# Head loads from two queues, small loads and constants later, and expert 0's W2 split moved behind attention

## The chip, the cores and the metric

One core of one Trainium2 chip. The time is that of the whole kernel on the device, in microseconds (us); of several runs the median is given, and one further execution is taken with the hardware profiler. Engines are called by their names or as the profile does: PE is TensorE's matmul, PEld its weight load, DVE VectorE, ACT ScalarE, POOL GpSimd, SP SyncE; a q behind the name is the engine's sequencer, which issues DMAs.

## The reference, cut to what matters

A linear attention with decay (state of 48 x 48 per head, 4 sequences of 768 tokens, 8 heads) gives x, and x goes through a mixture of 8 experts, two for each token:

```
for t in range(S):
    cur = einsum('bhd,bhe->bhde', u * k[t], v[t])
    y[t] = einsum('bhd,bhde->bhe', r[t], state + cur)
    state = w * state + einsum('bhd,bhe->bhde', k[t], v[t])
x = y as [3072, 384]
noisy = x @ w_gate + log1p(exp(x @ w_noise)) * noise
top 2 of 8 experts a token, weights by softmax over the two
out[token] += weight * (relu(x @ w1[e]) @ w2[e])     # w1 384 x 1024, w2 1024 x 384
```

All in float32.

## The kernel before, in words

**Attention.** 24 tiles of 128 tokens: step i of the loop `for i in range(NT)` handles chunk i // 4 of sequence i % 4. For a tile r and k are transposed and scaled by powers of w (`trans`; r's result is rT, multiplied on VectorE, k's is kT, copied on ScalarE), multiplied to scores (`scores`, line 415) and masked on VectorE onto a tile that holds the diagonal (`mask`, line 420). The diagonal is the sum of r k u over a head: GpSimd forms the product (`uterm_a`, two operations of 384 columns, lines 376 and 378), VectorE sums it (`uterm_b`, line 386), GpSimd and ScalarE write it into place (`diag`, a select on line 392 and four activations). GpSimd also prepares k for the state update (`prep_k`, two operations of 192 columns, line 370). `kvup` and `zadd` update the state, `inter` and `intra` (lines 464 and 477) multiply scores and state with r and v, `back` and `xout` transpose the result and store x to DRAM. Chunk 5 has no state update. Step i works on tile i and prepares i + 1 and i + 2.

**Order.** The kernel is scheduled by hand: each engine and each DMA queue runs its instructions in the order in which the program writes them. Loads are all issued by SyncE, `load(i + 4)` in step i; the program's first lines load tiles 0 to 2, u, the gate weights (`wg`, four small loads) and the noise (`nz`, four). `consts_a` writes small constants, on GpSimd and VectorE, ahead of the loop.

**Routing.** Every fourth tile's logits are taken (`logits`, line 520). The tokens fall into two groups, of tiles 0 to 12 and 13 to 23. When a group's logits are there, `route(g)` is queued: some hundred short VectorE operations, of which `rstep(us)` issues a measured share at two places in a step; what the first group works on is in PSUM where possible, the second group's operands are in SBUF. `consts_c` checks w (five VectorE operations on one partition) in steps 17 and 19. From the lists that come out GpSimd gathers rows of x by indirect DMA (`xgather`, line 982; `gate0` for the weights, line 1026).

**Experts.** A weight matrix is split into a high part (`w_hi`, ScalarE) and a low part, the matrix less the high part (`w_lo`, VectorE, line 345), and each product is made of three matmuls. Expert 0's seven blocks (three of W1 of 1024 columns, four of W2 of 768) pass through three staging buffers during attention. Block j is loaded in step `W0_AT[j] - 1`, split high in `W0_AT[j] + 2` and low in `W0_AT[j] + 3`:

```
W0_AT = (3, 6, 8, 10, 12, 14, 16)
W_LAG = 2
```

so loads are in steps 2, 5, 7, 9, 11, 13 and 15, high parts in 5 to 18, low parts in 6, 9, 11, 13, 15, 17 and 19. After attention `p1(0, 0)` (line 1080) and `p2(0, 0)` (line 1116) run expert 0 on its first three tiles of tokens, beside the second routing pass; then the other chunks and experts follow.

## Time and profile before

| | us |
|---|---|
| median of three runs | 590.85 (587.71 to 591.36) |
| the profiled execution | 582.96 |
| its span, first to last instruction | 581.2 |

| engine | busy us | share of the span | instructions |
|---|---|---|---|
| PE | 558.4 | 96% | 4460 |
| PEld | 526.7 | 91% | 4461 |
| DVE | 351.3 | 60% | 818 |
| POOL | 268.9 | 46% | 375 |
| ACT | 240.8 | 41% | 559 |

The span falls into the head (to about 28 us), attention (to about 140 us) and the experts. Matmuls are pipelined, so a busy PE need not be at its peak, and the granted clock of a stretch says at which of its speeds TensorE ran, 1.00 being full. The spans on POOL are rough. A share over the whole span is an average over stages with different limits.

### The profile page before, as it was taken

Reading aid. Unit: us, or ns where it says so; the run is one execution under the profiler, and the core shown is the slowest. Engines: PE = TensorE matmul, PEld = TensorE weight load, DVE = VectorE, ACT = ScalarE, POOL = GpSimd, SP = SyncE. Lnnn points to the kernel's source line nnn. Section 1 sums busy time; section 2 is a strip of 40 time slices with the busy share of each in tenths; the row PEclk is TensorE's granted clock in tenths of the full one; section 3 lists DMA queues with packets and bytes.
Section 4 is the critical chain, followed back from the end, with each engine's and each line's share of the span. In section 5 each row is a group of like instructions: output and inputs, shape, how many; then the busy total and the mean of one; then the engine's idle time right before and its main releaser. Section 6 shows DMA issues by size and latency. Waiting matters only on the chain.

```text
span 581.2 us, 12332 instructions
## 1 busy us (share of the span) xinstructions
PE 558.4 (96%) x4460; PEld 526.7 (91%) x4461; DVE 351.3 (60%) x818; ACT 240.8 (41%) x559; POOL 268.9 (46%) x375
## 2 busy tenths in 40 slices
PE   6999998989989999999999999999999999999995
PEld 3788886877979899999999999999999999999994
DVE  7567879968959885636373646455453745455330
ACT  3576767644225251524342444334342533434220
POOL 6789767672036375136322633371445146235102
PEclk9999999979999999999999999999999999999998
DMA  9999998747624266456553835483546448554101
GB/s 126 180 207 220 210 211 178 149 125 213 214 49 129 90 163 161 127 150 171 145 154 110 208 108 165 117 213 103 165 127 186 126 133 212 137 160 119 43 15 40
DMA packets 133816, 85.13 MB, mean 146 GB/s; under 512 B 109522, under 2 KB 123907, under 8 KB 133748
## 3 DMA queue, kind: packets, MB, share of 16 engines
q1 hardware_dynamic: 124196, 56.38, 41.3%
q0 software_dynamic: 9552, 27.89, 16.4%
q8 instruction: 37, 0.61, 0.5%
q14 instruction: 31, 0.25, 0.2%
HBM read 57.89 MB, written 19.37 MB: 133 GB/s over the span
## 4 chain that ended last, share of the span: by engine, by line
PE 83%; DVE 7%; SPq 2%; DMA 2%; issue 2%; POOL 1%; ACT 0%; POOLq 0%; DVEq 0%
PE ph L1080 34%; PE pym L1116 32%; PE pa L415 3%; PE yt L477 3%; PE pt L403 2%; PE yt L464 1%; SPq L135 1%; PE ptb L486 1%; DMA xg<-xd,GR 1%; DVE am L420 1%; PE pym L1107 1%; PE pym L1109 1%; PE pwarm L428 1%; PE pl L520 1%; DMA rd<-in_r_dram 1%
## 5 line engine op out<-in xcount | busy, mean ns | idle before, releaser
L1116 PE MATMUL pym<-w1h,hb 128*128 128x384 f32 x768 | 199.6, 336 | 0.0
L1116 PEld LDWEIGHTS pym<-w1h,hb 128*128 128x128 f32 x768 | 138.9, 188 | 0.1
L1080 PE MATMUL ph<-xh,w0h 128*128 128x384 f32 (+2 forms) x384 | 131.8, 343 | 0.7 <-ACT xh L1055 0.7
L1080 PE MATMUL ph<-xl,w0h 128*128 128x384 f32 (+2 forms) x384 | 131.5, 342 | 0.5 <-DVE xl L1056 0.5
L1080 PE MATMUL ph<-xh,w0l 128*128 128x384 f32 (+2 forms) x384 | 131.3, 342 | 0.0
L1116 PE MATMUL pym<-w1l,hb 128*128 128x384 f32 x384 | 128.9, 336 | 0.0
L1086 DVE SCALAR_TENSOR_TENSOR hb<-ph,hb 128x384 fp32r<-128x384 f32 x128 | 71.0, 555 | 92.2 <-ACT hb L1084 54.9
L1139 POOL DMA_INDIRECT out_dram<-ot,TK x53 | 55.7, 1051 | 138.0 <-DVE ot L1135 122.4
L1084 ACT ACTIVATE hb<-ph 128x384 fp32r<-128x384 f32 x128 | 63.0, 492 | 102.5 <-PE ph L1080 97.8
L1080 PEld LDWEIGHTS ph<-xh,w0h 128*128 128x128 f32 x384 | 72.2, 188 | 1.6 <-ACT xh L1055 0.9
L1080 PEld LDWEIGHTS ph<-xl,w0h 128*128 128x128 f32 x384 | 72.0, 188 | 1.2 <-DVE xl L1056 0.8
L1080 PEld LDWEIGHTS ph<-xh,w0l 128*128 128x128 f32 x384 | 72.1, 188 | 0.6
L1116 PEld LDWEIGHTS pym<-w1l,hb 128*128 128x128 f32 x384 | 72.1, 188 | 0.0
L982 POOL DMA_INDIRECT xgt<-xd,GR x39 | 39.4, 1011 | 68.8 <-DVE ht L1086 36.7
L991 POOL DMA_INDIRECT pv<-out_dram,GA x46 | 51.8, 1126 | 27.5 <-issue 15.4
L1124 ACT ACTIVATE ot<-pym 128x384 f32<-128x384 f32 x39 | 19.2, 492 | 92.6 <-PE pym L1116 80.9
L1056 DVE TENSOR_TENSOR xl<-xq,xh 128x384 fp32r<-128x384 f32 (+2 forms) x39 | 21.0, 539 | 33.9 <-ACT xh L1055 33.9
L420 DVE COPY_PREDICATED am<-mneg,pa 128x512 f32<-128x512 int32 x48 | 32.5, 730 | 13.5 <-PE pa L415 12.2
L1135 DVE SCALAR_TENSOR_TENSOR ot<-ot,GT,pv 128x384 f32<-128x384 f32 (+2 forms) x43 | 25.9, 610 | 16.3 <-ACT ot L1124 16.3
L1055 ACT ACTIVATE xh<-xq 128x384 fp32r<-128x384 f32 (+2 forms) x39 | 19.7, 505 | 32.4 <-DVE xq L1046 27.1
L397 ACT ACTIVATE am<-ident,c 128x128 f32<-128x128 f32 x96 | 30.4, 391 | 1.3 <-DVE c L386 1.3
L345 DVE TENSOR_TENSOR w1l<-stg,w1h 128x768 fp32r<-128x768 f32 x32 | 30.8, 964 | 0.0
(297 smaller groups left out, 766.7 us busy)
## 6 DMA issues: line engine op xcount, KB each, us to landing
stg<-in_moe_w_dram SPq DMA_DIRECT2D x32, 384.0 KB, 4.0
stg<-in_moe_w_dram SPq DMA_DIRECT2D x72, 128.0 KB, 4.1
xq<-xgt SPq DMA_DIRECT2D x176, 36.0 KB, 1.9
rd<-in_r_dram SPq DMA_DIRECT2D x24, 192.0 KB, 4.8
vd<-in_v_dram SPq DMA_DIRECT2D x24, 192.0 KB, 4.6
out_dram<-zrow SPq DMA_DIRECT2D x16, 288.0 KB, 4.6
kt<-in_k_dram SPq DMA_DIRECT2D x23, 192.0 KB, 4.0
stg<-in_moe_w_dram SPq DMA_DIRECT2D x6, 512.0 KB, 5.9
```

Source lines behind the costliest of these rows:

```text
L345: nc.vector.tensor_sub(lo, tv, hi.bitcast(F32))
L397: nc.scalar.activation(AM[i][:, 1, p, :], ident, AF.Copy, scale=C8[i][:, 1, p, :])
L420: nc.vector.copy_predicated(AM[i][:, s], mneg.to_broadcast([128, NP, 128]), PA[i][s])
L982: nc.gpsimd.indirect_dma_start(out=xg[:n], out_offset=None, in_=xd[:GROUPS[GEARLY - 1][1] * 128] if early_ else xd, in_offset=bass.Indirec ...
L991: nc.gpsimd.indirect_dma_start(out=pv[:n], out_offset=None, in_=out, in_offset=bass.IndirectOffsetOnAxis(ap=GA[:n, e * NJ + t:e * NJ + t + ...
L1056: nc.vector.tensor_sub(xl[:, g], v, xh[:, g].bitcast(F32))
L1080: nc.tensor.matmul(ph[:, :w_], a[:, d, fs], x[:, :w_ // 32, d], start=(j == 0), stop=(j == len(q) - 1))
L1084: nc.scalar.activation(h_[:, f, 0, :], ph[:, a:b], AF.Relu)
L1086: nc.vector.scalar_tensor_tensor(h_[:, f, 1, :], ph[:, a:b], 0.0, h_[:, f, 0, :].bitcast(F32), op0=ALU.max, op1=ALU.subtract)
L1116: nc.tensor.matmul(py, hb[:, f, a, hs], x[:, f, :], start=(j == 0), stop=(j == len(q) - 1))
L1135: nc.vector.scalar_tensor_tensor(ot[:n], pt[:n], g, PV[e, t][:n], op0=ALU.mult, op1=ALU.add)
L1139: st = nc.gpsimd.indirect_dma_start(out=out, out_offset=bass.IndirectOffsetOnAxis(ap=TK[:n, q:q + 1], axis=0), in_=ot[:n], in_offset=None, ...
```

## The change

1. Head: the second load of w, that of u and that of tile 0's r are issued by ScalarE, the rest by SyncE. u's broadcast (`pub`, `ub`) comes before the first transposes.
2. The gate weights are loaded in step 1, the noise in steps 8 to 11.
3. GpSimd's order ahead of the loop and in steps 0 to 3: k of tile 1 is prepared before that of tile 0, and in steps up to `HEAD` the product for tile i + 2 comes behind the select of tile i + 1 and the prepared k, not ahead of them. Its sum (`uterm_b`) comes behind the masks.
4. Six VectorE operations of `consts_a` go to the end of step 1 (`consts_b`).
5. The check of w goes from steps 17 and 19 to 8 and 10.
6. Expert 0's blocks have tables of their own: W1's are loaded in steps 4, 7 and 10, W2's in 18, 19, 20 and 22. W2's low parts are made by GpSimd, in steps 22 and 23 and, the last two, after the first step of `p1(0, 0)`, and so is the last high part, on ScalarE.

```
+W0_AT = {4: 0, 7: 1, 10: 2, 18: 3, 19: 4, 20: 5, 22: 6}
+W0_HI = {7: 0, 10: 1, 13: 2, 20: 3, 21: 4, 22: 5}
+W0_LO = {8: 0, 11: 1, 14: 2, 22: 3, 23: 4}
+HEAD = 3
+NZ_AT = 8
-FLAG_AT = 17
+FLAG_AT = 8
...
-        nc.sync.dma_start(wp[two * 64:two * 64 + D, :],
+        (nc.scalar if two else nc.sync).dma_start(wp[two * 64:two * 64 + D, :],
...
-    load(0, (0, 2))
+    load(0, (0, 1))
...
-    nc.sync.dma_start(ur, bass.AP(tensor=u.tensor, offset=u.offset, ap=[[0, 1], [1, H * D]]))
+    nc.scalar.dma_start(ur, bass.AP(tensor=u.tensor, offset=u.offset, ap=[[0, 1], [1, H * D]]))
+    load(0, (1, 2), nc.scalar)
     load(0, (2, 3))
     load(1)
     load(2)
...
-    def w_lo(e, k):
+    def w_lo(e, k, eng=None):
         if e < E:
             tv, hi, lo = w_view(e, k)
-            nc.vector.tensor_sub(lo, tv, hi.bitcast(F32))
+            (eng or nc.vector).tensor_sub(lo, tv, hi.bitcast(F32))
...
+    def consts_b():
+        nc.vector.tensor_scalar(ltri, idif, 0.0, None, op0=ALU.is_gt)
+        nc.vector.tensor_scalar(ier, ie, -1.0, float(E), op0=ALU.mult, op1=ALU.add)
+        nc.vector.tensor_scalar(ie_n[:, 0, :], ie, float(LS), None, op0=ALU.mult)
+        nc.vector.tensor_copy(pid[:, 0, :], ie[:1])
         nc.vector.tensor_copy(imp, im)
         nc.vector.tensor_copy(ijp, ij.rearrange("p e j -> p (e j)")[:, :NJ])
...
     consts_a()
     uterm_a(0)
-    uterm_a(1)
-    prep_k(0)
+    prep_k(1)
     uterm_b(0)
     diag(0, 0)
     diag(0, 1)
-    prep_k(1)
+    uterm_a(1)
+    prep_k(0)
     scores(0)
-    nc.vector.tensor_mul(RKU[1], RKU[1], ub)
     mask(0, 0)
     mask(0, 1)
-    uterm_b(1)
...
             trans(i + 1, 0)
-            if i + 2 < NT:
+            if HEAD < i < NT - 2:
                 uterm_a(i + 2)
+            if i == 0:
+                nc.vector.tensor_mul(RKU[1], RKU[1], ub)
+                uterm_b(1)
+                prep_k(2)
             diag(i + 1, 0)
             trans(i + 1, 1)
-            diag(i + 1, 1)
-        if i - W_LAG - 1 in W0_AT:
-            w_lo(0, W0_AT.index(i - W_LAG - 1))
+            if i:
+                diag(i + 1, 1)
+        if i in W0_LO and i < 20:
+            w_lo(0, W0_LO[i])
         inter(i)
         if i:
             logits(i - 1, wgs)
-        if i + 2 < NT:
+        if 0 < i < NT - 2:
             prep_k(i + 2)
+        if i <= HEAD:
+            uterm_a(i + 2)
         rstep(STEPS_A, False)
...
+        if i in W0_LO and i >= 20:
+            w_lo(0, W0_LO[i], nc.gpsimd)
...
-        kvup(i)
+        if i:
+            kvup(i)
         intra(i)
+        if i == 0:
+            diag(1, 1)
+            kvup(0)
         zadd(i)
-        if i + 2 < NT:
+        if HEAD < i < NT - 2:
             uterm_b(i + 2)
         if nxt:
             scores(i + 1)
             mask(i + 1, 0)
             mask(i + 1, 1)
+        if i <= HEAD:
+            uterm_b(i + 2)
+        if i == 1:
+            consts_b()
...
+        if i == 1:
+            load_wg()
+        if NZ_AT <= i < NZ_AT + B:
+            load_nz(i - NZ_AT)
...
-        if i + 1 in W0_AT:
-            w_load(0, W0_AT.index(i + 1))
+        if i in W0_AT:
+            w_load(0, W0_AT[i])
         back(i)
-        if i - W_LAG in W0_AT:
-            w_hi(0, W0_AT.index(i - W_LAG))
+        if i in W0_HI:
+            w_hi(0, W0_HI[i])
...
     fill(FILL)
+    w_lo(0, 5, nc.gpsimd)
+    w_hi(0, 6)
+    w_lo(0, 6, nc.gpsimd)
```

## Rows read from the trace of the kernel before

**Rows 1.** The chain that ended last, whole kernel: start us, us, what

```profile
15.78 4.76 DMA rd<-in_r_dram
...
29.42 0.89 PE yt L477 x16
...
57.97 0.99 PE yt L464 x16
...
62.90 0.60 PE yt L464 x16
...
119.27 1.98 PE yt L477 x16
...
165.07 4.59 DMA xg<-xd,GR
```

**Rows 2.** Busy us of each engine by stretch, clock, DMA share, GB/s

```profile
core 0: us, PE busy (x) PEld busy (x) DVE busy (x) ACT busy (x) POOL busy (x), PEclk, DMA share, GB/s
28.00:82.00 54.00, 53.95 (x925) 45.92 (x923) 39.30 (x69) 36.65 (x99) 45.94 (x59) 1.00 0.98 213
82.00:128.00 46.00, 40.43 (x643) 34.24 (x645) 41.63 (x102) 28.00 (x81) 31.63 (x45) 0.93 0.67 151
120.00:130.00 10.00, 10.00 (x135) 8.55 (x132) 5.13 (x13) 4.32 (x13) 8.46 (x12) 0.72 0.31 85
```

**Rows 3.** Timeline of the head, SyncE's queue: start us, us, engine, line, operation

```profile
10.38 1.34 SPq L151 DMA_DIRECT2D wg<-in_moe_w_gate_dram  x2
...
12.74 2.22 SPq L155 DMA_DIRECT2D nz<-in_moe_noise_dram  x4
```

**Rows 4.** Timeline of the head, the engines: start us, us, engine, line, operation

```profile
7.49 0.60 ACT L215 ACTIVATE tabk<-ptab 128x512 f32<-128x512 f32 x1 [0.98 <-PE ptab L212]
...
26.44 0.64 POOL L392 TENSOR_SCALAR_AFFINE_SELECT am<-c 128x512 f32<-128x512 f32 x1
26.53 0.55 DVE L386 TENSOR_REDUCE c<-rku 128x8 f32<-128x384 f32 x1 [0.69 <-POOL rku L378]
...
27.05 1.16 POOL L370 TENSOR_TENSOR kd<-kt,tabk 128x192 f32<-128x192 f32 x2
...
28.16 1.00 POOL L376 TENSOR_TENSOR rku<-rd,kt 128x384 f32<-128x384 f32 x1
...
30.19 0.64 POOL L392 TENSOR_SCALAR_AFFINE_SELECT am<-c 128x512 f32<-128x512 f32 x1
...
32.75 0.69 DVE L408 TENSOR_TENSOR rT<-pt,pwr 128x512 f32<-128x512 f32 x1
```

**Rows 5.** Timeline of the routing stage, VectorE, and TensorE behind it

```profile
101.50 1.18 DVE L345 TENSOR_TENSOR w1l<-stg,w1h 128x768 fp32r<-128x768 f32 x1
...
108.80 1.36 DVE L420 COPY_PREDICATED am<-mneg,pa 128x512 f32<-128x512 int32 x2 [0.16 <-PE pa L415]
...
113.28 0.94 DVE L345 TENSOR_TENSOR w1l<-stg,w1h 128x768 fp32r<-128x768 f32 x1
...
116.01 0.34 DVE L289 TENSOR_SCALAR stg<-stg 1x384 f32<-1x384 f32 x1
...
117.71 0.14 DVE L293 CAST tab<-bad 1x1 int32<-1x1 f32 x1
...
119.27 1.98 PE L477 MATMUL yt<-am,vd 128*64 128x128 f32 x16 [2.55 <-DVE am L420]
```

**Rows 6.** Timeline: a VectorE operation beside a GpSimd one, and again alone

```profile
110.51 1.00 POOL L378 TENSOR_TENSOR rku<-rku,ub 128x384 f32<-128x384 f32 x1
...
110.67 0.88 DVE L773 SCALAR_TENSOR_TENSOR r_s<-SLF,r_om 128x13 f32<-128x13 f32 x1
...
158.16 0.18 DVE L773 SCALAR_TENSOR_TENSOR r_s<-SLF,r_om 128x11 f32<-128x11 f32 x1
```

**Rows 7.** Timeline after attention: GpSimd's last gate gather, second routing pass, TensorE

```profile
143.54 0.95 POOL L1026 DMA_INDIRECT GT<-xd,GX  x1 [0.30 <-issue]
...
144.34 0.24 DVE L694 SCALAR_TENSOR_TENSOR r_p<-lg 128x88 f32<-128x88 f32 x1
...
157.25 0.20 PE L758 MATMUL pwarm<-r_om,ltri 128*128 128x88 bf16 x1
```

More of the change, by code (lines that the diff above doesn't have):

```diff
@@ L29 @@
 STEPS_KV = 0.42
-W0_AT = (3, 6, 8, 10, 12, 14, 16)
-W_LAG = 2
+W0_AT = {4: 0, 7: 1, 10: 2, 18: 3, 19: 4, 20: 5, 22: 6}
[3 more added lines that the diff above has]
+NZ_AT = 8
 FILL = 1
 STEPS_END = 0.9
-FLAG_AT = 17
+FLAG_AT = 8
 STEPS_P1 = 0.85
@@ L122, with load @@
     rt, kt, vt = {}, {}, {}
-    def load(i, part=(0, 3)):
+    def load(i, part=(0, 3), eng=None):
         c, b = divmod(i, B)
@@ L134, in load @@
                 t = kd[0][:, :, :D]
-            nc.sync.dma_start(t, src[b, :, c * C:(c + 1) * C, :].rearrange("h t e -> t h e"))
+            (eng or nc.sync).dma_start(t, src[b, :, c * C:(c + 1) * C, :].rearrange("h t e -> t h e"))
             dst[i] = t
-    load(0, (0, 2))
+    load(0, (0, 1))
     ub = const.tile([128, H, D], F32, name="ub")
@@ L148, with load_wg, load_nz @@
     nc.vector.memset(wg, 0.0)
-    for a, src in enumerate((w_gate, w_noise)):
-        for j in range(2):
-            nc.sync.dma_start(wg[j * 64:j * 64 + D, :, a * E:(a + 1) * E],
-                              src.rearrange("(j b d) e -> j d b e", j=2, d=D)[j])
-    nz = const.tile([128, NCH, B, E], F32, name="nz")
-    for b in range(B):
-        nc.sync.dma_start(nz[:, :, b, :], noise[b * S:(b + 1) * S, :].rearrange("(c p) e -> p c e", p=128))
-    nz = nz.rearrange("p c b e -> p (c b) e")
+    def load_wg():
+        for a, src in enumerate((w_gate, w_noise)):
+            for j in range(2):
+                nc.sync.dma_start(wg[j * 64:j * 64 + D, :, a * E:(a + 1) * E],
+                                  src.rearrange("(j b d) e -> j d b e", j=2, d=D)[j])
+    nz4 = const.tile([128, NCH, B, E], F32, name="nz")
+    nz = nz4.rearrange("p c b e -> p (c b) e")
+    def load_nz(b):
+        nc.sync.dma_start(nz4[:, :, b, :], noise[b * S:(b + 1) * S, :].rearrange("(c p) e -> p c e", p=128))
     zrow = const.tile([128, DM], F32, name="zrow")
@@ L197 @@
     nc.scalar.activation(pwr[:, :, 0:64], pwk[:, :, 127:63:-1], AF.Copy)
+    pub = psum.tile([128, H * D], F32, name="pub", tag="py0")
+    nc.tensor.matmul(pub, one_r, ur, start=True, stop=True)
+    nc.scalar.activation(ub.rearrange("p h d -> p (h d)"), pub, AF.Copy)
     kT, rT = {}, {}
@@ L212 @@
         nc.tensor.transpose(ptab[:, p, :], pwk[:, p, :], ident)
-    pub = psum.tile([128, H * D], F32, name="pub", tag="py0")
-    nc.tensor.matmul(pub, one_r, ur, start=True, stop=True)
     nc.scalar.activation(tabk.rearrange("p h d -> p (h d)"), ptab.rearrange("p a b -> p (a b)"), AF.Copy)
-    nc.scalar.activation(ub.rearrange("p h d -> p (h d)"), pub, AF.Copy)
     acc = const.tile([128, E], BF16, name="acc")
@@ L255, in consts_a @@
     def consts_a():
-        nc.vector.tensor_scalar(ltri, idif, 0.0, None, op0=ALU.is_gt)
         nc.gpsimd.memset(ones_b, 1.0)
@@ L263, in consts_a @@
         nc.gpsimd.iota(ie, pattern=[[1, E]], base=0, channel_multiplier=0, allow_small_or_imprecise_dtypes=True)
-        nc.vector.tensor_scalar(ier, ie, -1.0, float(E), op0=ALU.mult, op1=ALU.add)
-        nc.vector.tensor_scalar(ie_n[:, 0, :], ie, float(LS), None, op0=ALU.mult)
         nc.gpsimd.memset(dl, 0.0)
@@ L269, in consts_a @@
         nc.gpsimd.memset(cap[:, E - NS:], float(NM * 128))
-        nc.vector.tensor_copy(pid[:, 0, :], ie[:1])
         nc.gpsimd.iota(im, pattern=[[1, 128]], base=0, channel_multiplier=0)
```

## The prediction

> **What bounds the kernel now.** I read the chain of waits first, as it names the stage in which time can be won, then the busy times by stage, then the timeline of the two stages that the change touches. The chain has four stretches. Up to about 25 us it runs through the load queue: the r tile of step 3 is issued at 15.78 and lands 4.76 us later, and GpSimd stands still for it [rows 1]. From 28 to 82 us the chain is TensorE alone, one tile step in 4.5 us (57.97 to 62.90, less the 0.39 that part 2 explains) [rows 1]. From 82 to 122 us it is VectorE, on which the first routing pass runs beside attention; TensorE is busy 40.43 of 46 us there and its mean clock is 0.93 [rows 2]. After attention it goes to and fro between VectorE's second routing pass, a gather (165.07, 4.59 us) and expert 0's matmuls [rows 1], and from expert 1 on it is matmuls. The change can win only in the first and third stretch, and can lose in the second and fourth.
>
> **1. The head: -0.3 us.** The four small gate loads and the four noise loads hold SyncE's queue from 10.38 to 14.96 [rows 3]. They leave it, and the third tile's loads follow the others directly, so the r that landed at 20.54 should land near 16. The chain of GpSimd then decides, in its new order. The table of powers is ready at 8.09 [rows 4]. Behind it come, in the queue's order, prepared k of tile 1 (1.16), the select of tile 0 (0.64), r times k of tile 1 (1.00), prepared k of tiles 0 and 2 (2.3), the select of tile 1 (0.64); with gaps the product of tile 2 starts at about 14.4. From there every tile up to 5 is one round: in the old order a round, from select to select, takes 3.75 us (26.44 to 30.19), as the sum over the product is taken by VectorE while GpSimd does something else. In the new order the select waits right behind that sum, 0.55 us, and a dispatch, so a round takes 4.4 [rows 4]. Three rounds bring the product of tile 5 to 27.6, its second half and its sum to 30.2, and VectorE's rT of tile 5, which is queued behind that sum, to some 30.8, against 32.75 [rows 4]: a gain of 1.9. Against it stands the block of small constants that moves from before the tiles to step 1. Its four VectorE operations within SBUF come just when GpSimd works without a gap, and such an operation waits until GpSimd's running instruction is over (part 5): four waits of 0.4 to 1.0, about 2 us, of which I take 1.6 as lying on the chain, since rT of tile 3 and the masks are queued behind them. Net -0.3. Bounds: -3.0 (the constants find gaps, the product of tile 2 starts a microsecond earlier) and +2.0 (they find none, and TensorE, idle between the masks, drops to its lower clock for a tile). Issue on ScalarE's queue saves SyncE some 0.6 us an issue [rows 3], which is inside these 1.9; wp, u and r of tile 0 take ScalarE about 2 us ahead of its first activation, which waits for VectorE's scan anyway.
>
> **2. Tiles 4 to 13, TensorE's stretch: +0.8.** The check of w moves from step 19 to step 10, the low parts from 6, 9, 11 and 13 to 8 and 11. VectorE is busy 39.30 of 54 us here, so a tile has some 1.2 us to spare [rows 2]; a low part of W1 fits nearly, the check with its 1.84 us (116.01 to 117.85) [rows 5] and the waits for GpSimd, which is busy 45.94 of the 54 us [rows 2], doesn't. Behind it are queued the state update, the sum and the masks of tile 11, and for those TensorE waits. I take 0.8, between 0 (the spare of two tiles covers it) and +1.5. The high parts on ScalarE cost only beside a logits tile, where TensorE's first matmul of the step took 0.99 instead of 0.60 [rows 1]: two such before (steps 8 and 12), two after (13 and 21), nothing. The W2 loads that leave cost nothing either way: loads are not what ends the waits here.
>
> **3. The routing stage: -5.5.** Low parts leave steps 15, 17 and 19, one arrives at 14. VectorE has no idle time between 82 and 122 us but the 0.16 at 108.80, where it waits for the scores of tile 19 [rows 5]. So what is won before 108.80 is kept only as far as TensorE follows: the part at 14 takes the place of that at 15, and of the 1.18 at 101.50 I keep 0.7; that the new one lies a step earlier and is a W1 part costs 0.4. Between the masks of tiles 19 and 20 VectorE's queue loses 0.94 and 1.84 us [rows 5], 2.8, all on the chain: TensorE waits 2.55 us for the mask of tile 20 [rows 5]. Nearly all of that wait goes, and with it what follows it: the 16 matmuls take 1.98 instead of 0.89 [rows 1], TensorE at 1.2 GHz instead of 2.4, and the mean clock of 120 to 130 us is 0.72 with TensorE busy throughout [rows 2], so 5.6 of the 10 us went at half speed and cost 2.8. I take 2.4 back, as VectorE is then close behind TensorE. 0.7 - 0.4 + 2.8 + 2.4 = 5.5. Bounds: 3.0 (the clock falls all the same) and 7.0 (the waits of VectorE for GpSimd in step 19 shrink too).
>
> **4. Last tiles: +0.9.** High parts come to steps 20 to 22 on ScalarE, in steps that have no state update any more and are shorter; +0.3. Two low parts go to GpSimd behind the early gathers, 2.0 us each (768 columns at the 1.00 that 384 take) [rows 4]; the sixth W2 load waits for the first of them in SyncE's queue, ahead of the store of tile 22, which isn't ready then. If they meet VectorE's gate arithmetic, the rT and the mask of tile 23 are late by up to 1.9; most of that arithmetic reads PSUM, so I take 0.6. Bounds 0 and +2.5.
>
> **5. The low parts after attention: +3.2.** VectorE and GpSimd exclude each other when both work within SBUF: a VectorE operation on 13 elements takes 0.88 while a GpSimd product runs from 110.51 to 111.51, and 0.18 when GpSimd is idle; it ends 0.04 after GpSimd does [rows 6]. The last two low parts stand in GpSimd's queue behind the three gathers of gates, the last of which ends at 144.49. At 144.34 VectorE begins the second routing pass, whose operands, other than the first pass's, are all in SBUF, and it goes on without a pause till its one-hot matrix, for which TensorE's matmul at 157.25 is waiting [rows 7]. Behind that stand the list, the gather and its landing, all on the chain [rows 1]. So two instructions of 2.0 us stop VectorE for up to 4.0; less the moments in which it works from PSUM I take 3.2. Bounds 0 (VectorE always wins the port) and 4.0. The Trainium skill, "GPSIMD Engine Reference", section "Elementwise — side-by-side cycle accounting", has about 2.6 cycles an element at 1.2 GHz for a two-input operation; by it a part would take an estimated 1.7 us, this term 2.7 and the sum -1.4. No row here has that size on GpSimd, and the sum goes by the 1.00 of 384 columns.
>
> **Sum.** -0.3 + 0.8 - 5.5 + 0.9 + 3.2 = -0.9 us against the profiled execution's 582.96 (span 581.2 and 1.8 around it). That execution is 1.3% below the median of the timed runs, 590.85; the experts' matmuls, where the rest of the time is, don't change, so I set the same difference against the median: 590.0. One per cent, 5.9 us, is about what can be told from no change.
>
> **Rivals.** *The exclusion hardly bites* (0.28): the constants, the check and the low parts find VectorE working from PSUM or between operations. For it: most of VectorE's work in the routing stage reads PSUM and ran its usual time beside GpSimd. Against it: the row of 0.88. Then the head gives its 1.9 and part of the bound, -2.4, parts 2, 4 and 5 cost 0.2, 0.4 and 0.4, part 3 stays: -6.9, 584.0. *Slower, by the clock* (0.14): held up 4 us at 144.5, VectorE frees the PSUM buffers of expert 0's first chunk late, TensorE stands still over 2 us, and as at 119.27 its next matmuls run at 1.2 GHz. It decides if that standstill comes near the 2.55 us before tile 20 [rows 5]. Two or three microseconds of half speed in the first chunk and again before the gather, with the upper bounds of parts 1, 4 and 5: 2.0 + 0.8 - 5.5 + 2.5 + 4.0 + 3.0 = +6.8, 597.7. *The routing stage doesn't yield* (0.10): with less to do VectorE meets GpSimd's instructions oftener and the standstill at 119 us stays: part 3 gives 3.0, the sum is +1.6, 592.5.
>
> **How the numbers follow.** The forecast has 0.48, and its own range, from its bounds taken half together, is 586 to 594. The range of 584 to 596 takes in the first rival's time, though not what lies below it, and the third rival's; the slower one's is left out. Faster by over 1% (below 584.9): 0.24 of the first rival and 0.04 of the forecast, whose bounds of parts 3 and 5 reach there, 0.28. Slower by over 1% (above 596.8): most of the second rival, 0.12. Within 1%: 0.60.
>
> **What would show it.** Part 1: the first matmuls of tile 4's state product some 0.3 us from where they are, and the four constants in step 1 longer than alone. Part 3: no standstill of TensorE before tile 20, and its 16 matmuls near 0.9. Part 5: GpSimd's two parts of 2 us in the first chunk, and a VectorE operation of about 2 us beside each. Wrong, if those operations keep their 0.2, or if tile 4 starts over 3 us earlier.

## The result, and the profile after

| group of runs | kernel before, us | changed kernel, us | ratio, 95% interval |
|---|---|---|---|
| first comparison, 20 runs each | 588.81 | 583.49 | 0.9906 [0.9878, 0.9935] |
| A | 588.11 | 583.61 | 0.9932 [0.9902, 0.9962] |
| C | 595.24 | 587.77 | 0.9872 [0.9814, 0.9930] |
| D | 581.50 | 578.49 | 0.9957 [0.9943, 0.9972] |

The changed kernel is faster by 0.9% in the first comparison, 5.3 us by the medians. The forecast was 590.0 in a range of 584 to 596; the time lies 0.5 us below the range. The difference is within 1%, which the forecast held likeliest, in three of the four groups. The gain differs from group to group, and so does the level. The kernels of a group A to E ran on one chip, in turn; the expectations below call A the first group and B the second. B (before: 582.3) and E (581.9) timed other kernels. The kernel before against itself gave 1.0002 [0.997, 1.0034] in A, 1.0069 [0.9998, 1.0139] in C and 1.0020 [1.0001, 1.0040] in D, so C is worth the least; in D the interval leaves out 1 for the same program, so that 0.2% tells nothing there. In C 13 of the 17 runs of the kernel before lie over 1.5% above its fastest, the other four have a median of 589.12, and the ratio of 0.9872 does not follow from those four, so C gives no size of the gain. C and E ran on the same chip.

The profiled execution of the changed kernel took 584.21 us, span 582.5. From its page, the engines' busy times and TensorE's granted clock in 40 slices:

```profile
PE 555.9 (95%) x4460; PEld 523.2 (90%) x4461; DVE 351.5 (60%) x814; ACT 240.7 (41%) x559; POOL 274.0 (47%) x379
...
PEclk9999999999999999999999999999999999999998
```

The engines' totals barely move; what moved is when they work. The same stretches as in [rows 2] (columns as there):

```profile
28.00:82.00 54.00, 53.03 (x912) 45.15 (x910) 40.54 (x74) 35.16 (x96) 45.35 (x58) 1.00 0.97 200
82.00:128.00 46.00, 42.66 (x705) 35.63 (x705) 40.50 (x108) 30.01 (x89) 34.12 (x47) 1.00 0.78 191
120.00:130.00 10.00, 8.87 (x126) 7.23 (x124) 6.58 (x27) 6.04 (x16) 8.11 (x8) 1.00 0.79 235
```

Between 120 and 130 us the clock is 1.00 where it was 0.72 [rows 2]: the stage no longer has the standstill of TensorE that [rows 5] end with. Behind attention the opposite happened. GpSimd, VectorE and TensorE in the changed kernel's timeline (start, length, then engine, line, operation), which answer to [rows 7]:

```profile
137.95 3.65 POOL L354 TENSOR_TENSOR w1l<-stg,w1h 128x768 fp32r<-128x768 f32 x2
```

```profile
138.88 2.84 DVE L703 SCALAR_TENSOR_TENSOR r_p<-lg 128x88 f32<-128x88 f32 x1
```

```profile
143.72 0.45 PE L1089 MATMUL ph<-xh,w0h 128*128 128x384 f32 x1 [1.68 <-DVE hb L1095]
```

The first operation of the second routing pass takes 2.84 instead of 0.24 us and ends 0.1 us behind GpSimd's two low parts; one hidden-layer operation queued behind it is then late by 1.68 us for TensorE.

**A ledger of stages.** Five landmarks cut every profile into the prediction's parts: `intra` (the masked scores times v, line 477, in the changed kernel 486) of tiles 4, 17, 21 and 23, and the first instruction of the gather behind the second routing pass. The expectations below call `intra` of a tile its state product; their first matmul after the gather is the transpose of the third block of gathered rows. The rows of the kernel before in group D, and of the changed kernel in the same group (timeline of TensorE and of GpSimd; the chain of waits puts the products 0.1 to 0.2 us later):

```profile
35.15 1.06 PE L477 MATMUL yt<-am,vd 128*64 128x128 f32 x16
...
102.20 1.06 PE L477 MATMUL yt<-am,vd 128*64 128x128 f32 x16
...
119.68 1.28 PE L477 MATMUL yt<-am,vd 128*64 128x128 f32 x16 [2.55 <-DVE am L420]
125.63 1.09 PE L477 MATMUL yt<-am,vd 128*64 128x128 f32 x16
...
133.92 1.09 PE L477 MATMUL yt<-am,vd 128*64 128x128 f32 x16
...
160.57 0.95 POOL L982 DMA_INDIRECT xg<-xd,GR  x1 [17.79 <-DVE r_p L793]
```

```profile
32.16 1.06 PE L486 MATMUL yt<-am,vd 128*64 128x128 f32 x16
...
99.75 1.06 PE L486 MATMUL yt<-am,vd 128*64 128x128 f32 x16
...
120.01 1.09 PE L486 MATMUL yt<-am,vd 128*64 128x128 f32 x16
...
128.41 1.09 PE L486 MATMUL yt<-am,vd 128*64 128x128 f32 x16
...
159.14 0.96 POOL L991 DMA_INDIRECT xg<-xd,GR  x1 [17.30 <-DVE r_p L802]
```

Subtracted from each other, and the same for groups A and C and for the two profiles of the first comparison (changed minus before, us):

| stage (part of the prediction) | forecast | D | A | C | first |
|---|---|---|---|---|---|
| start to tile 4 (1) | -0.3 | -2.99 | -0.95 | -3.27 | -2.64 |
| tiles 4 to 17 (2, and 0.3 kept of 3) | +0.5 | +0.54 | +0.51 | +0.26 | +0.61 |
| tiles 17 to 21 (3) | -5.2 | -3.17 | -4.26 | -5.62 | -5.60 |
| tiles 21 to 23 (4) | +0.9 | +0.11 | -0.71 | -2.64 | +1.26 |
| tile 23 to the gather (5) | +3.2 | +4.08 | +3.19 | +3.21 | +3.53 |
| gather to the end of the span | 0 | -0.97 | -2.42 | +0.46 | +4.14 |
| sum, which is the difference of the spans | -0.9 | -2.4 | -4.6 | -7.6 | +1.3 |
| difference of the timed medians | | -3.0 | -4.5 | not usable | -5.3 |

(Of part 3's 0.7 - 0.4, put at steps 14 and 15, the table has 0.3 in the second line.) In D and A the profiles give the timed difference to within 0.6 us. The pair of the first comparison doesn't: the kernel before was profiled at 581.2 with 418.6 us behind the gather's first instruction, which is the level of group D (418.1 and 417.2), and the changed kernel at 582.5 with 422.8, the level of A and C (422.0 to 424.4).

### The profile page after: what moved, and what is told of

Same layout as the page of the kernel before. It is cut to its first block, busy times and chain, and to the rows that moved or that the text cites. A ratio compares the mean times of both kernels' runs of the same rounds, so it can differ in the third digit from the quotient of the medians.

```text
span 582.5 us, 12330 instructions
## 1 busy us (share of the span) xinstructions
PE 555.9 (95%) x4460; PEld 523.2 (90%) x4461; DVE 351.5 (60%) x814; ACT 240.7 (41%) x559; POOL 274.0 (47%) x379
## 4 chain that ended last, share of the span: by engine, by line
PE 80%; DVE 9%; POOL 3%; issue 3%; ACT 2%; DMA 2%; SPq 0%; another core or an unknown queue 0%; POOLq 0%; DVEq 0%; ACTq 0%
PE ph L1089 33%; PE pym L1125 32%; PE pa L424 3%; PE yt L486 2%; PE pt L412 2%; DVE am L429 1%; DMA xg<-xd,GR 1%; PE pl L529 1%; PE pym L1116 1%; PE pym L1118 1%; PE ptb L495 1%; PE yt L473 1%; PE pwarm L437 1%; DVE rT L417 1%; POOL kd L379 1%
## 5 line engine op out<-in xcount | busy, mean ns | idle before, releaser
L424 PE MATMUL pa<-rT,kT 64*128 64x128 f32 x384 | 27.9, 284 | 5.0 <-ACT hb L489 3.1
```

The lines of the kernel that those rows point to most:

```text
L424: nc.tensor.matmul(pa[s][:, p, :], kT[i][s * 64:(s + 1) * 64, p, :], rT[i][s * 64:(s + 1) * 64, p, :], start=True, stop=True)
```

## The experiments

**The same two kernels again.** No edit. Group A:

> The kernel before, unchanged, for a second profiled execution. Theory A (the profiled execution of the kernel before, 582.96 us, was quicker than a usual one, because its TensorE paused nowhere in the expert stage): a second one takes about 588 us, agrees with the first within 0.5 us up to the first matmul after the gather (169.8 us), and is longer behind it, by pauses of TensorE of 0.8 to 2 us that the profile puts to issue. Theory B (the first profile was usual and what follows the gather is the same in every execution): about 583 us and no pauses. Ratio to the kernel before 1.000 under both.

> The changed kernel, unchanged, for a second profiled execution. Theory A (the gain up to the gather is 2.7 us, and executions differ by pauses of TensorE in the expert stage whatever the kernel): first matmul after the gather again within 0.5 us of 167.1; the rest, 415.4 us in the first profile against 411.4 in the kernel before, comes out anywhere between the two. Theory B (the change itself makes the expert stage longer): again 415 us for the rest. Ratio to the kernel before 0.990 under both, about -5.5 us.

Measured: spans 588.4 and 583.8. In the kernel before the first matmul after the gather starts at 169.71, as in the first profile, and everything behind it takes longer, as in theory A, though not by the pauses that theory A names (see the end of the next section). The changed kernel missed the expected 167.1 at that matmul by 2 us (169.25), of which 1.6 are the head's (below). Group C:

> The kernel before, unchanged. In the first group of runs its median was 588.1 us, in the second 582.3, and the profile that the prediction was set against, 582.96, looks like the second (391.8 us from the first matmul after the gather to the last batch of matmuls; 392.0 to 392.1 in all four profiles of the second group, 394.5 to 399.0 in those of the first). Theory: the level belongs to the group of runs, not to the kernel: this profile's stretch behind the gather agrees with the level of this group's median (392 with 582, 395 or more with 588). Rival: the kernel before has the longer stretch by itself now and then: 392 to 399 whatever the median.

> The changed kernel, unchanged, for a profile beside one of the kernel before on the same chip. Theory (the gain is what the traces show at the gather, 0.5 to 2.7 us, and the further 2 to 3 us of the first group come from pauses of TensorE in the expert stage, which that group had and the second hadn't): in a group with the kernel before at 582, ratio 0.995 to 0.999; in one with it at 588, 0.990 to 0.993 as twice before. Rival (the changed kernel is 5 us faster everywhere): ratio 0.991 in either.

Measured: spans 591.4 and 583.8. From the first matmul after the gather to the last batch the kernel before takes 395.8 us, which is the level of A, as the theory had it; but that is not all that makes this execution long: here the kernel before lost time ahead of the gather, with that matmul at 175.06. The chain of waits of that profile, in the head, TensorE in the 2 us that begin at 26 (us, busy us, clock, DMA share, GB/s), and TensorE's timeline in the step of tile 21 (the brackets: idle time before, and what ended it):

```profile
15.67 5.59 DMA rd<-in_r_dram
...
26.39 1.73 PE yt L477 x16
```

```profile
26.00:28.00 2.00, 2.00 (x26) 0.50 1.16 191
```

```profile
131.57 0.31 PE L477 MATMUL yt<-am,vd 128*64 128x128 f32 x1 [0.21 <-issue]
131.82 1.10 PE L415 MATMUL pa<-rT,kT 64*128 64x128 f32 x9
133.08 0.59 PE L415 MATMUL pa<-rT,kT 64*128 64x128 f32 x5 [0.16 <-issue]
```

The load of [rows 1] takes 5.59 instead of 4.76 us here, and the 16 matmuls behind it 1.73 instead of 0.89, as TensorE stood still for 2.70 us and then ran at 1.2 GHz; in step 21, while an early gather runs, TensorE gets its instructions in pieces, and from 136 to 138 us its clock is 0.50 again. The new head's chain has no load at that place, and its tile 4 is at 33.88 in C as in A (33.90). Group D:

> The kernel before, unchanged. Theory (the first profile was quick in the last attention tiles): from the state product of tile 17 to that of tile 23 it takes 34.7 us or more (34.1 in the first profile; 34.7, 34.9 and 38.1 in the old routing stage's other profiles; 28.6 to 29.9 in all profiles with the new one), and the first matmul after the gather starts at 169.7 us or later. Rival (what is missing lies behind the gather): 34.1 and 169.7, and over 395 us behind it where the changed kernel of the same group has 392 to 395.

> The changed kernel, unchanged. Theory: 28.6 to 29.9 us from tile 17 to tile 23 and 167.0 to 169.3 at the first matmul after the gather, as in three profiles, so that the kernel before of the same group is 1 to 5 us later there; ratio to the kernel before 0.985 to 0.995, the lower the later it is. Rival: the difference at the gather stays under 1.5 us and the timed one is 4 us or more.

Measured: 31.7 us from tile 17 to 23 in the kernel before (34.7 or more expected), gather's matmul at 166.30, ratio 0.9957, spans 578.7 and 576.3. The changed kernel reached that matmul at 164.85, earlier than expected too, so the two are 1.45 us apart there and 3.0 in time: neither theory nor rival of the last text. The ratio is where the theory of group C's second text had it for a kernel before at 582 (0.995 to 0.999). So the theory that the first profile was unusually quick in the last tiles falls: there are executions quicker still. What is left of it: the old routing stage takes 31.7 to 38.1 us in five profiles (four of this kernel, one with the new head), the new one 28.6 to 30.4 in all fifteen.

**The two halves of the change.** The head alone, with the constants below put back:

```diff
-W0_AT = {4: 0, 7: 1, 10: 2, 18: 3, 19: 4, 20: 5, 22: 6}
+W0_AT = {2: 0, 5: 1, 7: 2, 9: 3, 11: 4, 13: 5, 15: 6}
...
-FLAG_AT = 8
+FLAG_AT = 17
...
-    w_lo(0, 5, nc.gpsimd)
-    w_hi(0, 6)
-    w_lo(0, 6, nc.gpsimd)
```

> The change of the head alone: the loads, GpSimd's order in tiles 0 to 3 and the small constants as in the changed kernel; the loads, high and low parts of expert 0 and the check of w at the steps of the kernel before, all low parts on VectorE. Theory (as the two traces read): the key-value products of tile 4 start at 31.9 us instead of 34.6, the first matmul after the gather comes 2.0 to 2.6 us before 169.8, the time falls by 2 to 2.6 us (ratio 0.996). Rival (the prediction's own step: the four constants held by GpSimd eat the gain): 34.3 us and a time within 0.5 us of the kernel before (0.999). A second rival: what is won before tile 4 is lost before the gather, because VectorE's routing stage ends at its own time: 31.9 us, but 169.5 at the gather and a ratio of 1.000.

Measured: tile 4 at 33.91, 0.9 us before that of its group; 1.0 us ahead at tile 23 (136.03 against 137.03), 0.25 at the gather's first instruction, ratio 1.0006 [0.9968, 1.0044], medians 586.31 and 588.11. Between theory and rivals: the head gave a third of what the first profile showed, and most of that was lost between tile 23 and the gather (27.74 us against 26.98), why isn't shown. With the rest of the change it is no more: in group A the whole change starts the gather at 161.80, the rest alone (next) at 162.12.

The other half is the kernel before with the changed kernel's tables `W0_AT`, `W0_HI`, `W0_LO`, `FLAG_AT = 8` and the three lines behind attention:

```diff
-W0_AT = (3, 6, 8, 10, 12, 14, 16)
...
+W0_AT = {4: 0, 7: 1, 10: 2, 18: 3, 19: 4, 20: 5, 22: 6}
...
-FLAG_AT = 17
+FLAG_AT = 8
...
+    w_lo(0, 5, nc.gpsimd)
+    w_hi(0, 6)
+    w_lo(0, 6, nc.gpsimd)
```

> The other half alone: the head as in the kernel before; the loads, high and low parts of expert 0, the check of w and the four low parts on GpSimd as in the changed kernel. Theory (the prediction's steps 2 to 5, with what the traces show of them): +0.2 to tile 13, -5.2 at the routing stage (the state product of tile 20 without its standstill, that of tile 21 at about 122.5 instead of 127.7), +1.2 in the last tiles, +3.7 behind the gates: the first matmul after the gather within 0.5 us of 169.8 and the time within 1 us of the kernel before (ratio 1.000). Rival (the two low parts behind attention cost little, the timed gain of 5.5 us comes from the routing stage): the gather 3 us earlier, ratio 0.994.

Measured: 29.05 us from tile 17 to 23 (34.72 in the kernel before of the group), 30.72 from there to the gather (26.99), first matmul after it at 167.93, ratio 0.9957 [0.9926, 0.9989]. Both signs are as forecast, -5.7 and +3.7. The theory's zero came from the last tiles: it had -5.2 to tile 21 and +1.2 from there, measured are -4.2 and -1.4.

**The low parts behind attention.** On VectorE instead:

```diff
-    w_lo(0, 5, nc.gpsimd)
+    w_lo(0, 5)
     w_hi(0, 6)
-    w_lo(0, 6, nc.gpsimd)
+    w_lo(0, 6)
```

> The changed kernel with its last two low parts (5 and 6, behind attention) on VectorE instead of GpSimd, at the same place of the program. Theory (the two GpSimd instructions hold one VectorE operation for 2.84 us, and all of it is on the chain; the prediction's step 5): VectorE loses two operations of 0.94 to 1.18 us instead, no VectorE operation of 88 columns takes over 0.3 us, and the stretch from the last state product of attention to the first matmul after the gather, 37.5 us in both profiles of the changed kernel, takes 36 to 36.6. Time 1 to 1.5 us under the changed kernel's (ratio to the kernel before near 0.989). Rival (that operation waits for something else that ends at the same moment, or the stretch is set by another engine): the stretch stays at 37.5 or grows by the 1.9 us of the two operations to 39.4.

> The changed kernel with low parts 5 and 6 on VectorE, a second time, now beside the changed kernel itself. Theory (part 5's 3.2 us is all of the difference): 27.4 us from the last state product to the gather's first instruction, 30.1 to 30.7 in the changed kernel; time 2.5 to 3.5 us under the changed kernel's of this group. Rival (the first time it was the group of runs): within 1 us of it.

Measured: ratio 0.9916 [0.9886, 0.9947] in group B, where the changed kernel with a later matmul of u had 0.9969; 0.9922 [0.9904, 0.9940] in D, beside 0.9957 for the changed kernel itself; 0.9898 [0.9868, 0.9928] in E. From tile 23 to the gather 27.5 us in all three (30.2 to 30.7 in the changed kernel's four profiles). The timeline of VectorE in the first:

```profile
137.46 1.81 DVE L354 TENSOR_TENSOR w1l<-stg,w1h 128x768 fp32r<-128x768 f32 x2
139.19 0.55 DVE L1095 SCALAR_TENSOR_TENSOR hb<-ph,hb 128x384 fp32r<-128x384 f32 x1
139.66 0.16 DVE L637 COPY L<-pwarm 128x14 f32<-128x14 f32 x1
139.73 0.24 DVE L703 SCALAR_TENSOR_TENSOR r_p<-lg 128x88 f32<-128x88 f32 x1
```

Both low parts take 1.81 us together, partly where VectorE had been idle, and the operation that took 2.84 is back at 0.24. So 2.7 to 3.2 us of the loss on the chain were the hold, and the rival is out; the stretch of the expectation takes 33.2 us, so the hold cost more than its 36 to 36.6 allow. The kernel before has 26.65 to 26.98 from tile 23 to the gather: 0.5 to 0.9 us stay with the parts on VectorE. In time D gives 1.5 us by the medians, 2.0 by the ratios, less than the 2.5 to 3.5 expected: this profile had the slower start (tile 4 at 33.88, 1.7 us behind the changed kernel's in D).

Next, all of it ahead of the gathers of the gates:

```diff
         if not nxt:
+            w_lo(0, 5, nc.gpsimd)
+            w_hi(0, 6)
+            w_lo(0, 6, nc.gpsimd)
             until(gated, 0)
...
-    w_lo(0, 5, nc.gpsimd)
-    w_hi(0, 6)
-    w_lo(0, 6, nc.gpsimd)
```

> The changed kernel with low part 5, high part 6 and low part 6 moved ahead of the gathers of the gates in the last step of attention, where GpSimd is idle for 5.5 us, still on GpSimd and ScalarE. Theory (the hold of VectorE behind attention is the whole of the loss there): the stretch from the last state product to the first matmul after the gather falls from 37.5 to about 34 us, as in the kernel before (33.8 and 32.6), the GpSimd parts hold VectorE for 1 us or less ahead of it, and the time is about 3 us under the changed kernel's (ratio to the kernel before near 0.986). Rival (the hold only moves: the parts now meet the first routing pass's last operations, and the gates come late by as much): the stretch stays within 1 us of 37.5 and the time within 1 us of the changed kernel's.

Measured: ratio 0.9969 [0.9946, 0.9992]; from tile 23 to the gather 29.95 us, so 0.2 to 0.8 of the 2.7 to 3.2 us are won. The stretch of the expectation takes 35.7 us, between the theory's 34 and the rival's 36.5, and the rival's mechanism is what the rows show. VectorE's and ScalarE's timelines in the last step of attention:

```profile
128.91 2.12 DVE L806 TENSOR_SCALAR r_dn<-r_e 128x13 f32<-128x13 f32 x1
```

```profile
132.00 0.84 ACT L349 ACTIVATE w1h<-stg 128x768 fp32r<-128x768 f32 x1 [3.92 <-DMA stg<-in_moe_w_dram]
```

The first operation of the gates that works within SBUF is held until GpSimd's third low part ends (130.99), and ScalarE stands still 3.92 us for the load of block 6, with what makes the expert's input queued behind it.

**The check of w back in the routing stage:**

```diff
-FLAG_AT = 8
+FLAG_AT = 17
```

> The changed kernel with the check of w back at steps 17 and 19; the low parts stay out of the routing stage. Theory (the prediction's step 3 in its parts: the check costs its own 1.84 us there, and the standstill of TensorE that it makes costs up to 2.4 us of clock): from the state product of tile 17 to that of tile 21, 20.15 us in the changed kernel, 25.9 in the kernel before, it takes 22 us if TensorE keeps its clock and 24.4 if it falls; against that 0.6 us are won in tiles 10 to 12. Time 1.4 to 3.8 us over the changed kernel's. Rival (it was the low part in step 19 that tipped the stage, the check alone is covered): 20.2 to 20.8 us, and a time as the changed kernel's or 0.6 us under it.

Measured: 22.01 us from tile 17 to 21, against 20.25; TensorE waits for the mask of tile 20 again (waits: sum, number and longest, us):

```profile
PE yt L486 <- DVE am L429: 1.7, 1, 1.7
```

and keeps its clock, 1.00 in the four microseconds behind. So the check's own 1.84 us is 1.76 on the chain, as the theory had it without the clock's part. Tiles 4 to 17 take 67.13 us, 0.5 less than in the changed kernel of group D, though one kernel with the check at its new steps has 67.18 as well. Ratio 0.9977 [0.9954, 1.0001], the median 580.96 beside 580.36 for the one with u's matmul last: the 1.4 us of the theory don't show in time, and group B has no run of the changed kernel itself.

**The small constants back ahead of the tiles:**

```diff
     consts_a()
+    consts_b()
...
-        if i == 1:
-            consts_b()
```

> The changed kernel with the six small constants of VectorE back ahead of the tiles, as in the kernel before. The prediction's step 1 put 1.6 us on them in step 1. Theory (as the traces read it: three of the four find GpSimd idle, one is held to 0.62 us, and it runs beside GpSimd's select): tile 4's state product begins within 0.4 us of the changed kernel's, counted from the table of powers (23.8 us behind the start of GpSimd's first product with that table), and the time is the changed kernel's. Rival (the prediction): 1.6 us earlier from that point.

Measured: GpSimd's first product with the table starts at 10.19 and tile 4 at 33.93, 23.74 us apart, 23.69 to 23.84 in the changed kernel. The rival, which is the prediction's step, is out: their place costs nothing. The time, ratio 0.9833 [0.9742, 0.9924] in group C, decides nothing.

**The matmul of u in the head.** In the changed kernel it runs ahead of the transposes of k and r. Put behind all of them, as in the kernel before:

```diff
-    pub = psum.tile([128, H * D], F32, name="pub", tag="py0")
-    nc.tensor.matmul(pub, one_r, ur, start=True, stop=True)
-    nc.scalar.activation(ub.rearrange("p h d -> p (h d)"), pub, AF.Copy)
...
+    pub = psum.tile([128, H * D], F32, name="pub", tag="py0")
+    nc.tensor.matmul(pub, one_r, ur, start=True, stop=True)
     nc.scalar.activation(tabk.rearrange("p h d -> p (h d)"), ptab.rearrange("p a b -> p (a b)"), AF.Copy)
+    nc.scalar.activation(ub.rearrange("p h d -> p (h d)"), pub, AF.Copy)
```

> The changed kernel with the matmul that spreads u over the partitions put back behind the 12 transposes of the head, where the kernel before has it. In one profile of the changed kernel TensorE did the 4 transposes of r in 0.63 us and the state product of tile 4 began at 32.43; in the second, and in that of the head alone, they took 1.06 us, the table of powers came 1.8 us later, and tile 4 began at 34.07. Theory (with that matmul, which reads one partition only, as the first one behind the warm-up, TensorE comes to its full rate later in some executions; with the transposes first it is there by 7.2 us, as in three profiles of the old head): transposes of r at 0.6 to 1.0 us, tile 4 at 32.4 to 32.9. Rival (it is chance which rate TensorE has at 5 us, whatever stands first): 34.0 in some executions, this one among them or not. Time up to 1.1 us under the changed kernel's.

Measured: transposes at 0.63, as expected, but tile 4 at 33.32: GpSimd's select then waits 1.07 us for what needs u. Ratio 0.9969 [0.9949, 0.9989]. Put between those of k and those of r, with both late low parts on VectorE:

```diff
...
+        if nm == "kT":
+            pub = psum.tile([128, H * D], F32, name="pub", tag="py0")
+            nc.tensor.matmul(pub, one_r, ur, start=True, stop=True)
+            nc.scalar.activation(ub.rearrange("p h d -> p (h d)"), pub, AF.Copy)
...
```

> The changed kernel with low parts 5 and 6 on VectorE (as in the run that took 4.8 us off the kernel before), and the matmul that spreads u put between the transposes of k and those of r. Theory: the transposes of r take 0.63 us, as TensorE has its full rate by then, and u is there 1 us earlier than where the kernel before has it, so the state product of tile 4 begins at 32.4 (33.9 in four of six profiles of the new head, 33.3 with the matmul behind all transposes); from the last state product to the gather's first instruction 27.4 us; time 4.8 to 6 us under the kernel before (ratio 0.990 to 0.992). Rival (the rate at that moment is chance): tile 4 at 33.9, ratio 0.992.

> Low parts 5 and 6 on VectorE, the matmul of u between the transposes of k and of r; second profile. Theory (the place of that matmul decides the rate at which TensorE comes out of its warm-up): the four transposes of r 0.66 us or less and tile 4 at 32.6, as in the first. Rival (chance): 1.06 us and tile 4 at 33.9, as in seven of ten profiles with the matmul ahead of both. Time up to 1.2 us under late_vector_3's.

> The same kernel as best_2, for a third profile. Theory: transposes of r 0.66 us, tile 4 at 32.6 again. Rival: 1.06 us and 33.9 in this or the other one.

> Low parts 5 and 6 on VectorE, the matmul of u ahead of the transposes; third profile. Both theories: transposes of r 1.06 us and tile 4 at 33.9 more likely than 0.63 us and 32.3 (seven to three so far). Time 4.5 us under the kernel before (ratio 0.992).

The first profile of this kernel (group C, 587.04) has the transposes of r at 0.66 and tile 4 at 32.63. TensorE's timeline in late_vector_3 and in best_3:

```profile
5.09 1.64 PE L208 MATMUL pub<-stg 1*128 1x384 f32 x2
6.66 1.11 PE L214 MATMUL pt<-ident,kd 128*128 128x128 f32 x4
7.57 1.06 PE L214 MATMUL pt<-ident,rd 128*128 128x128 f32 x4
```

```profile
4.95 0.68 PE L211 MATMUL pt<-ident,kd 128*128 128x128 f32 x4
5.56 0.91 PE L217 MATMUL pub<-stg 1*128 1x384 f32 x2
6.72 0.63 PE L211 MATMUL pt<-ident,rd 128*128 128x128 f32 x4 [0.25 <-DMA rd<-in_r_dram]
```

With that matmul first, the transposes of r take 1.06 us in eight of eleven profiles and tile 4 starts at 33.9; in three they take 0.63 and it starts at 32.2 to 32.4. With k first they take 0.66 or less in all three of this kernel, tile 4 at 32.2 to 32.6. The place matters, and chance remains: in the six profiles with that matmul last the transposes of r take 0.63 us in four, 0.81 and 1.01 in two. In time it shows nothing: 577.18 (ratio 0.9908 [0.9879, 0.9938]) beside 576.54 (0.9898) in E, though the spans of the profiles are 573.7 and 573.9 against 574.7. The low parts on VectorE beat both kernels; for the matmul of u, 1 us is not decided.

## Why the prediction was right and wrong

**Part 1, -0.3: wrong, mis-sized by 0.7 to 3 us.** The walk through GpSimd's queue was right: the product of tile 2 forecast at 14.4 started at 14.37, and a round forecast at 4.4 took 4.54 between these selects of the changed kernel:

```profile
17.18 0.64 POOL L401 TENSOR_SCALAR_AFFINE_SELECT am<-c 128x512 f32<-128x512 f32 x1 [0.72 <-DVE c L395]
...
21.72 0.63 POOL L401 TENSOR_SCALAR_AFFINE_SELECT am<-c 128x512 f32<-128x512 f32 x1 [0.75 <-DVE ltri L281]
```

Two things failed. The step "four waits of 0.4 to 1.0, about 2 us, of which I take 1.6 as lying on the chain" was wrong: VectorE runs the constants in the 0.75 us in which GpSimd stands idle for the same sum, and only the fourth is held:

```profile
21.48 0.22 DVE L281 TENSOR_SCALAR ltri<-stg 128x128 bf16<-128x128 int32 x1
21.61 0.17 DVE L282 TENSOR_SCALAR ier<-ie 128x8 f32<-128x8 f32 x1
21.68 0.16 DVE L283 TENSOR_SCALAR ie_n<-ie 128x8 f32<-128x8 f32 x1
21.76 0.62 DVE L284 CAST pid<-ie 1x8 int32<-1x8 f32 x1
```

The prediction had that 0.55 us gap and the dispatch in its own round, and did not put the constants into it. The run with the constants moved back shows the price: none. And three rounds are one too many for tile 4. The forecast's own end point came out without the constants, VectorE's rT of tile 5, forecast at 30.8:

```profile
30.99 0.68 DVE L417 TENSOR_TENSOR rT<-pt,pwr 128x512 f32<-128x512 f32 x1
```

But tile 4 doesn't wait for it: the chain of waits leaves GpSimd at the sum of 21.01 and is TensorE's from 23.51 on, so the third round's 0.65 isn't paid. Together 2.3 us more than forecast, which is what the first profile shows (-2.64). What the prediction did not have is TensorE's rate at 5 us: in eight of eleven profiles it takes 1.65 us of this back. And the old head pays more where its load is late and the clock falls behind it (tile 4 at 37.15 in C), which one profile could not show. How much of all this reaches the end is not settled: the head alone has a ratio of 1.0006, and 0.25 us are left of it at the gather.

**Part 2, +0.8, with the 0.3 kept at steps 14 and 15: right**, +0.3 to +0.6 against +0.5. That the check of w at its new step is most of it isn't shown: moved away, the stretch takes 67.13 us, and kernels with the check there take 67.2 to 68.1.

**Part 3, -5.5: right in mechanism, and right against the profile it was worked out from** (-5.6 from tile 17 to 21 in the first pair). The check is 1.76 of it, as measured alone. What the runs add is that the clock's part, forecast at 2.4 from one profile, is not fixed. The same standstill of 2.55 us stands before tile 20 in every profile of the kernel before. Behind it TensorE's clock, in windows of 2 us that begin with the standstill (us, busy us, clock, DMA share, GB/s), in group D and in group A:

```profile
117.68:119.68 2.00, 0.00 (x0) 1.00 0.82 232
119.68:121.68 2.00, 2.00 (x28) 1.00 0.19 64
```

```profile
117.79:119.79 2.00, 0.00 (x0) 0.94 0.82 231
119.79:121.79 2.00, 2.00 (x18) 0.50 0.19 64
```

In D it stays at 2.4 GHz; in A it is at 1.2 GHz for some 3 us, in the first profile and in C for some 6. So the part is worth 3.2 us in D, where no clock was lost, and up to 5.6 where some 6 us were; the 2.4 between them is the forecast's size. With the last tiles it is 3.1 to 8.3.

**Part 4, +0.9: right only against the first profile** (+1.26), and there by another cause: TensorE waits 0.37 and 0.54 us for ScalarE in that profile and not in D's, while GpSimd's low parts hold next to nothing (last section). The stretch from tile 21 to 23 varies more by itself: 8.4 to 9.6 us in the changed kernel, 8.3 to 12.3 in the kernel before.

**Part 5, +3.2: right**, +3.2 to +4.1 (bound 4.0), in place, in size and in cause: 2.7 to 3.2 of it are the hold. One detail differs: not several operations but one is held, through both of GpSimd's instructions. They took 1.83 us each, between the 2.0 that was scaled from 384 columns and the estimate of 1.7 that was worked out from the Trainium skill, "GPSIMD Engine Reference", section "Elementwise — side-by-side cycle accounting". By the Trainium skill's figure the term would have been 2.7; what was measured is 3.2 and more.

**The rivals.** The first, "the exclusion hardly bites", gave 584.0, which is nearest to the measured 583.49, and that is luck in the main. For the constants it was right. For the low parts its mechanism is refuted: the hold costs 2.7 to 3.2 us, as the runs with those parts on VectorE show. It left out that cost, and its base was 2.0 us too high. The second, "slower, by the clock", happens in part: TensorE waits 1.7 to 2.2 us behind the hold, and in three of the profiles its clock falls. In the run with u last (windows of 2 us, columns as above) and in the changed kernel of group D:

```profile
144.00:146.00 2.00, 1.29 (x4) 0.66 1.01 266
146.00:148.00 2.00, 2.00 (x8) 0.50 0.94 356
```

```profile
142.00:144.00 2.00, 0.85 (x5) 1.00 1.19 276
144.00:146.00 2.00, 2.00 (x13) 1.00 0.84 266
```

Its price is nothing there: tile 23 to the gather takes 30.70 us with the fall and 30.73 without, since VectorE's routing pass, not TensorE, leads to the gather. The third did not happen: no standstill before tile 20 is left.

**The sum, its base, and the step that failed.** 590.0 was 590.85, the median of three runs, less 0.9. The median of 20 is 588.81, which is 2.0 of the miss of 6.5 us. The other 4.4 is the change, -5.3 by the medians instead of -0.9. In the quiet group D it is -2.4 by the spans: there the head is 2.7 larger than forecast, part 3 and 4 together 1.2 smaller, part 5 0.9 larger, and 1.0 comes from behind the gather. So two steps failed. In the head, the constants' 1.6 us on the chain are none, and the third round's 0.65 isn't paid. And the zero for everything behind the gather measured -1.0 in D and -2.4 in A; its cause stays open, and with it two fifths of the gain in D and half of it in A. In A and C the kernel before loses more than the changed one: in the old head and the old routing stage (C), or behind the gather (A). That the last belongs to the change isn't shown: the stretch from the gather on, whose program is the same in all kernels here, takes 422.0 to 428.3 us in the four profiles of group C. In the kernel before of group A TensorE waits there for gathered rows and then runs at 1.2 GHz (its timeline, and a window of 2 us):

```profile
192.58 0.55 PE L1053 MATMUL ptm<-ident,xg 128*128 128x128 f32 x3 [1.69 <-DMA xg<-xd,GR]
```

```profile
196.00:198.00 2.00, 2.00 (x8) 0.50 0.00 0
```

The changed kernel of C loses its clock at the same place, that of A doesn't. The largest of TensorE's pauses in this stretch, in the run with the constants moved back, for which the profile shows no wait (issue):

```profile
282.11 0.45 PE L1125 MATMUL pym<-w1h,hb 128*128 128x384 f32 x1 [3.03 <-issue]
```

No pause of TensorE that is put to issue and longer than 0.5 us stands behind the gather in the profiles of B, D and E, though E ran on the chip of C; but none in the kernel before of A and the changed kernel of C either, so such pauses alone don't make the level. What makes them stays open.

## What to carry to other kernels

Take the base of a forecast from many executions and two profiles at least, and ask of every stage how much of its time is a standstill whose price (the clock behind it, a late load) varies: removing the routing stage's standstill was worth 3.2 us in one group and 5.6 in another. That isn't the chip alone: C and E ran on the same one, with medians of 587.04 and 577.18 for one and the same kernel. Ask also whether what is won early is still there at the next wait: 0.9 us in the head were 0.25 at the gather. Where an engine waits in a fixed rhythm, as GpSimd does for each tile's sum here, put small work of the other engine into that gap before pricing its conflict. Work moved to an idle engine isn't free if it holds a port that the engine on the critical path needs; here 1.8 us of work on the busy engine cost about 3 us less than 3.65 us on the idle one.

## What the runs showed of the hardware

- A VectorE operation that works within SBUF was held through two GpSimd instructions that ran back to back, 2.55 to 4.28 us for an operation of 0.2, and didn't get in between them. The Trainium skill, "SBUF — State Buffer", section "SBUF: two separate sides", has it that of a GpSimd operation and a VectorE one that has two SBUF inputs or runs in a two-port mode, the one that starts first holds the shared pair "for the whole instruction". The trace agrees as to the hold (2.84 beside 3.65), and adds that the second instruction of a pair came first again. In the longest hold, in the changed kernel of group D, the VectorE operation starts before the low parts (138.19) and while GpSimd issues a gather; why it was held already then isn't shown:

```profile
137.63 4.28 DVE L557 TENSOR_SCALAR r_n<-r_p 128x88 f32<-128x88 f32 x1
```

- Beside the two earlier low parts of GpSimd (3.59 us for the pair) VectorE's small operations on PSUM ran their usual 0.16 to 0.18; the longest hold was 0.37 instead of 0.17 us, for the first operation within SBUF that met them.
- After the warm-up (the program's first matmuls, which compute nothing that is used) TensorE took 1.06 us for r's transposes, which take 0.63 in other executions, in eight of eleven profiles in which a matmul that reads one partition came first. With k's transposes first, those took 1.08 to 1.09 in five of nine, and r's behind them never more than 1.01. The granted clock in the rows is 1.00 in both, so the rows don't show which level it ran at.
- A standstill of 2.5 us left the clock at 2.4 GHz in one profile and brought it to 1.2 GHz in the four others, one of 2.1 to 2.2 us did so in three of four: the length of the standstill alone doesn't tell.
